# One written-out issue order for all engines over all eight batches, with loads held on named VectorE operations

## The chip, the cores and the metric

The kernel runs on one core of a Trainium2 chip. The metric is the device time of one execution in microseconds, the median of several. The profile shows one execution, with its own time.

## The reference

Attention without softmax, per batch (8) and head (8), with 576 positions and 64 features per head, and then a gated long convolution with a projection on either side. What is computed, in short:

```python
def phi(x, c, s):
    r = np.maximum(x, 0.0)
    return np.concatenate([r * c, r * s], axis=-1)
q_p, k_p = phi(q, cos_w, sin_w), phi(k, cos_w, sin_w)
kv = np.einsum('bhsf,bhsd->bhfd', k_p, v)
num = np.einsum('bhsf,bhfd->bhsd', q_p, kv)
den = np.einsum('bhsf,bhf->bhs', q_p, k_p.sum(2))[..., None] + 1e-06
x = (num / den).transpose(0, 2, 1, 3).reshape(B, S, H * D)
...
x1, x2, x3 = split(x @ w_proj)
x2_conv = irfft(rfft(x2, axis=1) * rfft(filter_fft, axis=0))
out = (x1 * x2_conv * x3) @ w_out
```

Inputs and output are fp32. All matmuls run in fp16 with fp32 sums.

## The kernel before

Every batch goes through the same steps. In the order of its data: loads of q, k and v (512 KB and 64 KB of each, cast to fp16 by transfers that POOL issues, into six buffers `raw`); phi, the features qp and kp (VectorE, DVE: one instruction of 2560 columns and five of 512 for q, ten of 512 for k); va, v beside ones (ScalarE, ACT, or DVE); kv (TensorE, PE); qt, the transpose of qp into the one buffer qpt (for batches 0 and 1 on PE, from batch 2 on by DMA transposes that SyncE, SP, issues); num (PE) with the division to att (DVE), in four parts of two heads; xt, the transpose of att (for batch 0 on PE, then by one DMA transpose on SP); fx (PE, evicted by ACT), which folds att for the projection to x2; x2 (PE, evicted to x2f by ACT) in three parts; dft, the transform of x2 by a table, in three parts of 32-column matmuls (PE), evicted to xf (ACT) and multiplied by the filter's spectrum (DVE: m, m, yf); the gate, in four parts, for each x0 and x2s (two groups of eight matmuls of 288 columns, each pair evicted by ACT) and their product g (DVE); inv, the inverse transform (PE, evicted to eq by ACT); y (six DVE operations for each of four parts: eo twice, y twice, times g, ye); out (PE, evicted to os by ACT) and its transfer on SP.

PE's results stand in PSUM tiles of one tag, "u", with four buffers, so a group of matmuls starts when the eviction of the fourth group before it has read its tile.

What sets the order is the code in two parts. The setup (tables by sines, the filter's spectrum h) and batches 0 to 2 are written out call by call in a manual schedule, where instructions stand as they are written. Then a loop from batch 2 on emits the steps of batch b, with num, xt and fx of b+1 and loads, phi, qt, va and kv of b+2 between them (the names `n` and `n + 1` in the code); `behind` puts phi and va of the next batch behind a marked instruction of this one in the issue order. A whole step is emitted at a time: `emit_qt(n + 1, x)` for four x puts four transposes side by side on SP, and `emit_input_dma` three loads side by side on POOL. Each part of x2 is followed by its eviction at once, and in the loop the matmuls of dft stand behind it.

Names in the rows: L574 is x2's matmul, L592 its eviction, L613 dft, L645 the gate, L505 num, L477 the transpose of qp, L553 that of att, L110 a feature of 512 columns, L142 the load of 512 KB, L683 to L693 y, L404 and L417 the filter's matmuls, L712 out.

Of the kernel before, what the change touches and what calls it, by code (L numbers as in the profile page):

```python
# [17 lines left out]
def kernel(  # L18
# [30 lines left out]

    A1 = 2048.0  # L50
# [47 lines left out]
    v32 = work.tile([128, NH, NJ * D], FP32, tag="qp", bufs=2, name="v32")  # L98
    qpt_buf = const("qpt", [128, NH, SP_], FP16)
    va_buf = [const(f"va{i}", [128, NH, NJ, 66], FP16) for i in range(2)]  # L100
    raw_buf = [const(f"raw{i}", [128, NH, NJ * D], FP16) for i in range(6)]

# [3 lines left out]
    def tsc(out, in0, s1, op0, s2=None, op1=None):  # L106
        if op1 is None:
            return nc.vector.tensor_scalar(out=out, in0=in0, scalar1=s1, scalar2=None, op0=op0)
        else:
            return nc.vector.tensor_scalar(out=out, in0=in0, scalar1=s1, scalar2=s2, op0=op0, op1=op1)  # L110
# [12 lines left out]
    def behind(*key):  # L123

        return tc.issue_after(mark[key].ins) if key in mark else nullcontext()


    raw_t = {}
    raw_n = [0]
    XT_DMA = (1, 2, 3, 4, 5, 6, 7)  # L130
    DMA_QT = 2

    def load_qk(b, nm, hs=slice(0, NH), after=None):
        src = {"q": q, "k": k, "v": v}[nm]
        if hs.start == 0:
            raw_t[(b, nm)] = raw_buf[raw_n[0] % len(raw_buf)]
            raw_n[0] += 1
        rw = raw_t[(b, nm)]
        load_rows(nc.gpsimd, rw, src, b, hs, after)

    def load_rows(queue, rw, src, b, hs, after=None):
        first = queue.dma_start(  # L142
            out=rw[:, hs, 0 : 4 * D],
            in_=src[b, hs, 0:NM].rearrange("h (p j) d -> p h (j d)", j=4),
        )
        mark["load", b] = queue.dma_start(
            out=rw[0:64, hs, 4 * D : 5 * D], in_=src[b, hs, NM:S].rearrange("h p d -> p h d")
        )

        if after:  # L150
            hold(first, after)

    def hold(ins, key):

        tc.add_manual_dep(
            ins.ins, mark[key].ins.name,
            mybir.DependencyInfo(mybir.DependencyClass.Sync, mybir.DependencyReason.DATA),
            reason="hold",
        )

    def emit_va(b, xs=range(4), copy=nc.scalar.copy):
        for x in xs:
            hs = slice(2 * x, 2 * x + 2)
            copy(
                out=va_buf[b % 2][:, hs, :, 0:D],
                in_=(raw_t[(b, "v")] if b else v32)[:, hs].rearrange("p h (j d) -> p h j d", j=NJ),
            )

    def emit_input_dma(b, after=None):
        load_qk(b, "q", after=after)  # L170
        load_qk(b, "k")
        load_qk(b, "v")

    def load_wp(w):
# [5 lines left out]
    def load_filter():  # L180
# [6 lines left out]
    def load_wo():  # L187
        nc.gpsimd.dma_start(out=wo16, in_=moe_w_out.rearrange("(i p) n -> p i n", p=128))

# [6 lines left out]
    def emit_iotas(part):  # L196
        if part < 0:
# [3 lines left out]
            ])  # L201
            return
        if part == 0:
# [3 lines left out]
            iota("er_i", [128, 4, 16], lambda t: [(t, [[1, 4], [4, 16]], 0, 0)])  # L207
            return
# [9 lines left out]
        iota("sr_i", [128, QS], lambda t: [(t, [[2, 2], [8, QS // 2]], 1, 0)])  # L218

    def emit_cols():  # L220
        nc.vector.memset(half_pi, PI / 2.0)
        nc.scalar.activation(
# [3 lines left out]
        p = cc["p"] = small("p")  # L226
        nc.vector.tensor_copy(out=p, in_=cc["p_i"])
        nc.vector.memset(v32[64:128, :, 4 * D : 5 * D], 0.0)
        for r in raw_buf[0:2]:
            nc.vector.memset(r[64:128, :, 4 * D : 5 * D], 0.0)  # L230
        for va in va_buf:
            nc.vector.memset(va[:, :, :, D : D + 2], 1.0 / A1)
        nc.vector.memset(warm, 0.0)
        m = cc["m"] = small("m")
        rnd(m, p, 1.0 / 16.0, -15.0 / 32.0)
        lo = small("lo")
        stt(lo, m, -16.0, p)
        m8 = small("m8")
        tsc(m8, m, 1.0 / 9.0, AL.mult, -8.0 / 9.0, AL.add)
        ph = small("ph", 8).rearrange("p (k c) -> p k c", c=2)  # L240
        tsc(ph, cc["kr_i"], m8, AL.mult)
        tsc(ph[:, :, 0], ph[:, :, 0], 0.25, AL.add)
        rr = small("ph_r", 8).rearrange("p (k c) -> p k c", c=2)
        tsc(rr, ph, RC, AL.add, -RC, AL.add)
        nc.vector.tensor_tensor(out=ph, in0=ph, in1=rr, op=AL.subtract)
        coef = small("coef", 9)
        nc.vector.memset(coef[:, 8:9], 1.0)
        nc.scalar.activation(
            out=coef[:, 0:8], in_=ph.rearrange("p k c -> p (k c)"), func=AF.Sin, scale=TWO_PI
        )  # L250
# [30 lines left out]
    def cos_of(dst, m):  # L281
# [3 lines left out]
        nc.scalar.activation(out=a, in_=m, func=AF.Abs, bias=m_half[0:nr])  # L285
        nc.scalar.activation(
# [3 lines left out]
    def emit_rows():  # L290
# [27 lines left out]
        mk = cc["mk"] = small("mk", 8)
# [445 lines left out]
    for w in (0, 2, 1):  # L764
        load_wp(w)
# [205 lines left out]
```

## Time and profile before

| | us |
|---|---|
| median of 3 timed runs | 273.61 (272.73 to 273.91) |
| the profiled execution | 275.25 |
| its span in the trace | 273.4 |
| its mean granted clock of PE | 0.926 |
| PE busy | 222.1 (81%) |
| DVE busy | 198.4 (73%) |
| ACT busy | 165.7 (61%) |
| POOL busy | 48.0 (18%) |

The span is the time from the first instruction to the last in the trace; the execution's own time has 1.85 us more around it. Busy times are sums over all stages. The share of an engine that bounds one stage is read from the windows, since the setup, the first batches, the steady batches and the end have different limits. The granted clock is given as a share of the full 2.4 GHz.

### The profile page before, as it was taken

The page shows a single profiled execution, that of the slowest core. Times are in us where ns is not written, and L with a number is a line of the kernel's source. Part 1 is how long each engine was busy: PE and PEld are TensorE (multiplying, and loading weights), DVE is VectorE, ACT ScalarE, POOL GpSimd, SP SyncE. Part 2 cuts the span into 40 slices and gives each one's busy share as a digit, 9 for nine tenths or more (in the row PEclk, how much of TensorE's full clock was granted, in tenths as well). Part 3 has the DMA queues.
Part 4 walks back from the last instruction along what each step waited for, and adds up shares of the span by engine and source line. Part 5 has one row for each costly group of instructions (what it writes and reads, how often), then busy time and mean ns, then how long its engine had stood idle before and what let it go on. Part 6 is the DMA issues. An engine that isn't in the chain of part 4 may idle for free.

```text
span 273.4 us, 5930 instructions
## 1 busy us (share of the span) xinstructions
PE 222.1 (81%) x2282; PEld 145.6 (53%) x2282; DVE 198.4 (73%) x665; ACT 165.7 (61%) x256; POOL 48.0 (18%) x75
## 2 busy tenths in 40 slices
PE   2755987869995840446999999999999999999990
PEld 0344865644684520213776686577658657745840
DVE  4988567997399990515788979897897868456661
ACT  2255599484963540022695778588677948857731
POOL 8933500201810281100024022000000000000000
PEclk9989799997998995575999999999999999999997
DMA  7999998099998499999587999996596134042204
GB/s 142 212 206 193 199 192 118 7 181 193 144 191 103 111 212 164 147 156 196 114 86 122 235 147 162 272 191 152 174 198 95 56 119 98 0 173 80 78 19 173
DMA packets 95612, 39.70 MB, mean 145 GB/s; under 512 B 63648, under 2 KB 91296, under 8 KB 95584
## 3 DMA queue, kind: packets, MB, share of 16 engines
q0 software_dynamic: 38464, 16.26, 49.1%
q1 hardware_dynamic: 56752, 22.49, 39.9%
q10 hardware_dynamic: 368, 0.59, 0.6%
q8 instruction: 17, 0.28, 0.4%
q14 instruction: 11, 0.09, 0.1%
HBM read 33.69 MB, written 9.44 MB: 158 GB/s over the span
## 4 chain that ended last, share of the span: by engine, by line
PE 57%; DMA 15%; DVE 13%; ACT 11%; issue 2%; SPq 1%; POOL 0%; DVEq 0%; ACTq 0%; POOLq 0%
PE x L645 20%; PE x L574 10%; PE out L712 9%; DMA qpt<-qp 9%; PE dft L613 3%; DMA v<-in_v_dram 3%; PE kv L465 3%; DVE att L515 3%; PE fx L532 3%; ACT x2f L592 2%; PE inv L662 2%; PE inv L666 2%; DMA raw<-in_k_dram 2%; PE num L505 2%; PE out L718 1%
## 5 line engine op out<-in xcount | busy, mean ns | idle before, releaser
L645 PE MATMUL x<-xt,wp 128*128 128x288 f16 x512 | 69.5, 292 | 0.7 <-ACT x0s L650 0.4
L645 PEld LDWEIGHTS <-wp 128*128 128x128 f16 x512 | 50.4, 100 | 16.4 <-issue 3.4
L592 ACT ACTIVATE x2f<-x 128x1024 f16<-128x1024 f32 (+1 forms) x24 | 21.1, 885 | 36.4 <-PE x L574 36.4
L574 PE MATMUL x<-wp,fx 128*128 128x512 f16 (+1 forms) x160 | 39.0, 410 | 2.2 <-ACT fx L543 1.7
L505 PE MATMUL num<-kvs,qpt 128*128 128x65 f16 x320 | 15.7, 203 | 23.7 <-DMA qpt<-qp 19.1
L712 PE MATMUL out<-wo,y 128*128 128x512 f16 x128 | 30.6, 387 | 2.6 <-ACT os L740 2.3
L652 DVE TENSOR_TENSOR g<-x0s,x2s 128x576 f16<-128x576 f16 x32 | 14.6, 455 | 22.0 <-ACT x2s L650 22.0
L505 PEld LDWEIGHTS <-qpt 128*128 128x128 f16 x320 | 13.4, 103 | 29.9 <-DMA qpt<-qp 21.2
L515 DVE TENSOR_TENSOR att<-num,rcp 128x640 f16<-128x640 f32 x32 | 26.4, 824 | 0.8
L650 ACT CAST x2s<-x 128x576 f16<-128x576 f32 x32 | 20.6, 643 | 10.5 <-PE x L645 10.5
L650 ACT CAST x0s<-x 128x576 f16<-128x576 f32 x32 | 20.6, 644 | 7.4 <-PE x L645 6.0
L511 DVE TENSOR_TENSOR rcp<-num,epsc 128x10 f32<-128x10 f32 x32 | 5.1, 161 | 25.9 <-PE num L505 25.6
L574 PEld LDWEIGHTS <-fx 128*128 128x128 f16 (+1 forms) x160 | 13.5, 105 | 19.5 <-issue 6.8
L615 ACT CAST xf<-dft 128x1024 f16<-128x1024 f32 (+1 forms) x24 | 18.9, 812 | 7.3 <-PE dft L613 7.3
L672 ACT CAST eq<-inv 128x576 f16<-128x576 f32 x32 | 18.5, 672 | 4.6 <-PE inv L666 4.6
L712 PEld LDWEIGHTS <-y 128*128 128x128 f16 x128 | 12.4, 99 | 15.1 <-issue 2.1
L142 POOL DMA_DIRECT2D raw<-in_q_dram x9 | 10.5, 1163 | 54.5 <-DVE qp L110 39.0
L662 PE MATMUL inv<-itab,yf 128*128 128x144 f16 x128 | 16.9, 232 | 2.8 <-DVE att L515 2.8
L543 ACT CAST fx<-fx 128x576 f16<-128x576 f32 x30 | 18.7, 647 | 0.0
L683 DVE TENSOR_TENSOR eo<-eq 128x288 f16<-128x288 f16 x64 | 17.6, 303 | 1.3 <-ACT eq L672 1.3
L743 ACT ACTIVATE os<-out 128x1024 f32<-128x1024 f32 x14 | 14.5, 1039 | 6.3 <-PE out L712 5.5
L465 PE MATMUL kv<-va,kp 128*128 128x65 f16 x320 | 13.2, 197 | 5.1 <-DVE kp L110 1.9
(156 smaller groups left out, 406.3 us busy)
## 6 DMA issues: line engine op xcount, KB each, us to landing
out_dram<-os SPq DMA_DIRECT2D x30, 256.0 KB, 2.8
raw<-in_q_dram POOLq DMA_DIRECT2D x7, 512.0 KB, 11.8
raw<-in_k_dram POOLq DMA_DIRECT2D x7, 512.0 KB, 11.6
raw<-in_v_dram POOLq DMA_DIRECT2D x7, 512.0 KB, 11.5
wp<-in_moe_w_proj_dram POOLq DMA_DIRECT2D x3, 512.0 KB, 10.1
v<-in_v_dram SPq DMA_DIRECT2D x2, 512.0 KB, 5.5
out_dram<-os SPq DMA_DIRECT2D x15, 64.0 KB, 4.1
filt<-in_moe_filter_fft_dram POOLq DMA_DIRECT2D x2, 288.0 KB, 12.6
```

Source lines behind the costliest of these rows:

```text
L465: nc.tensor.matmul(u[:, h // 4, ds((h % 4) * 65, 65)], kp[:, j, h].rearrange("p a b -> p (a b)"), va[:, h, j, 0:65], start=(j == 0), stop= ...
L505: nc.tensor.matmul(u[:, hh, ds(t * 65, 65)], qpt_buf[:, h, ds(t * 128, 128)], kvs[:, h // 4, ds((h % 4) * 65, 65)], start=True, stop=True,)
L515: mark["att", b, hp] = nc.vector.tensor_tensor(out=att[:, hp].rearrange("p t (h d) -> p h t d", h=2), in0=nv[:, :, :, 0:D], in1=rcp.unsque ...
L543: mark["fx", b] = copy(out=fx[:, c].rearrange("p (v t a) -> p t v a", t=4, a=16), in_=uf.rearrange("p (t v a) -> p t v a", t=4, a=16)[:, : ...
L574: nc.tensor.matmul(dst, fx[:, c, ds(128 * ch, n)], wp16[:, c, ds(DM, DM)], start=(c == cs[0]), stop=(c == cs[-1]),)
L592: mark["x2f", b, bl] = nc.scalar.mul(out=x2f[:, 2 * bl : 2 * bl + n], in_=u[:, 0:n], mul=X2SC)
L615: mark["xf", b, bl] = nc.scalar.copy(out=xf, in_=u[:, :, 0:n])
L645: nc.tensor.matmul(u[:, hf, 0:HS], wp16[:, i, ds(w * DM + c * 128, 128)], xt[:, i, ds(HS * hf, HS)], start=(i == 0), stop=(i == NC - 1),)
L650: mark[f"x{w}s", b, c] = nc.scalar.copy(out=x, in_=u[:, :, 0:HS])
L662: nc.tensor.matmul(u[:, comp, ds(par * QS, QS)], yf[par][:, comp, ds(c * 128, 128)], itab[:, par + 4 * comp], start=(par == 0), stop=False,)
L672: mark["eo", b, c] = nc.scalar.copy(out=eq.rearrange("p a b c -> p a (b c)"), in_=u[:, :, 0:HS])
L712: nc.tensor.matmul(u[:, x], y[:, c, ds(QS * t, 128)], wo16[:, c], start=(c == 0), stop=(c == NC - 1),)
```

## The change

The loop, the marks and `behind` go. Each step becomes a generator that yields after each instruction or small group (a group of matmuls, an eviction, one DVE operation), and one text of words says which generator goes on next, over all eight batches and the setup:

```diff
+    def run(plan, **batch):
+        for word in plan.format(**batch).split():
+            word, _, n = word.partition("*")
+            word, _, which[0] = word.partition("'")
+            key = word.lstrip("~")
+            name = key.rstrip("0123456789.")
+            if key not in open_steps:
+                open_steps[key] = step[name](*(int(x) for x in key[len(name) :].split(".") if x))
+            held[0] = last_dve[0] if word[0] == "~" else None
+            for _ in range(int(n or 1)):
+                next(open_steps[key])
```

`dft1.0` is one step of dft of batch 1, part 0; `*3` three steps; `'v` and `'a` put an eviction or a feature on DVE or ACT. A load with `~` waits for the DVE operation that was emitted last:

```diff
+    def load_rows(queue, rw, src, b, hs):
+        to = slice(0, rw.shape[1]) if rw.shape[1] < NH else hs
+        first = queue.dma_start(
+            out=rw[:, to, 0 : 4 * D],
+            in_=src[b, hs, 0:NM].rearrange("h (p j) d -> p h (j d)", j=4),
+        )
+        if held[0] is not None:
+            tc.add_manual_dep(
+                first.ins, held[0].ins.name,
+                mybir.DependencyInfo(mybir.DependencyClass.Sync, mybir.DependencyReason.DATA),
+                reason="hold",
+            )
...
-    for b in range(2, B + 1):
...
-        if n + 1 < B:
-            emit_input_dma(n + 1)
-            with behind("g", b - 1, NC - 1):
-                emit_phi(n + 1, "q")
-            for x in range(4):
-                emit_qt(n + 1, x)
...
+    run("""
+        Sk0.0 io1 io0 io2 pad0 pad3 pad2 cols ones0 th cols pk0.0 pk0.0'a pk0.0 th'v Lq0.0
...
+        pr1.1 dft1.2 dft1.0 kv2.2 dft1.2 ~Lq4.2 y0.2*3 pq3.2 dft1.2 y0.2 dft1.0 dft1.2 ga1.1
...
+        out7.2.1 out7.1.1*2 out7.0.1 y7.3 out7.0.1 out7.1.1 out7.2.1*3 out7.1.1*3
+    """)
```

(`pr` is x2, `ga` and `gb` are the two groups of the gate, `xp` is the PE transpose of att of batch 0, `S` a load on SP, `L` one on POOL.) Fifteen loads are held: v, q and k of batch 3, v, q, k of 4, v, k, q of 5, q, v, k of 6 and q, v, k of 7. The first halves of k and v of batch 0 come as fp32 by SP, into k32 and v32, and some of batch 0's features go to ACT. The narrow matmuls (the 64-column part of x2, the 32-column ones of dft, the 64-column part of out) are placed next to each other. The last batch's out is cut in two, so that both last groups of a part are issued before its eviction. Instructions: PE 4566 to 4554, DVE 612 to 602, ACT 250 to 261, POOL 75 to 76, SP 43 to 52.

What the change does to SP's queue, around the transposes of batches 3 and 4 (qp_1521 and qp_1933 before). Before:

```order
L745 DMA out_dram<-os_3_1482 128x512 x2
L733 DMA out_dram<-os_4_1511 64x256 x2
L477 DMA_TRANSPOSE qpt<-qp_1521 128x10x128 x4
L477 DMA_TRANSPOSE qpt<-qp_1933 128x10x128 x4
L553 DMA_TRANSPOSE xt_1721<-att_1630 128x20x128
L745 DMA out_dram<-os_1_1968 128x512 x2
L745 DMA out_dram<-os_3_1981 128x512 x2
L733 DMA out_dram<-os_4_1994 64x256 x2
L477 DMA_TRANSPOSE qpt<-qp_2383 128x10x128 x4
```

After, where qp_1238 is batch 3's and qp_1490 batch 4's:

```order
L570 DMA_TRANSPOSE qpt<-qp_1238 128x10x128 x4
L847 DMA out_dram<-os_0_1355 128x512 x2
L847 DMA out_dram<-os_0_1782 128x512 x2
L653 DMA_TRANSPOSE xt_1921<-att_1833 128x20x128
L570 DMA_TRANSPOSE qpt<-qp_1490 128x10x128
L837 DMA out_dram<-os_4_1641 64x256 x2
L570 DMA_TRANSPOSE qpt<-qp_1490 128x10x128
L847 DMA out_dram<-os_1_1377 128x512 x2
L570 DMA_TRANSPOSE qpt<-qp_1490 128x10x128 x2
L847 DMA out_dram<-os_1_1812 128x512 x2
```

Four transposes of a batch stand by themselves now with an out or two between them; before, those of batches 3 and 4 were eight in a row.

POOL's queue, from the load of w_out on (raw_ is one of the six buffers). Before:

```order
L188 DMA wo_87<-in_moe_w_out_dram 128x4x512
L142 DMA raw_100<-in_q_dram 128x8x256
L146 DMA raw_100<-in_q_dram 64x8x64
L142 DMA raw_97<-in_q_dram 128x8x256
L146 DMA raw_97<-in_q_dram 64x8x64
L142 DMA raw_98<-in_k_dram 128x8x256
L146 DMA raw_98<-in_k_dram 64x8x64
L142 DMA raw_99<-in_v_dram 128x8x256
L146 DMA raw_99<-in_v_dram 64x8x64
```

After:

```order
L193 DMA wo_87<-in_moe_w_out_dram 128x4x512
L149 DMA raw_98<-in_v_dram 128x8x256
L159 DMA raw_98<-in_v_dram 64x8x64
L149 DMA raw_96<-in_q_dram 128x8x256
L159 DMA raw_96<-in_q_dram 64x8x64
L149 DMA raw_100<-in_k_dram 128x8x256
L159 DMA raw_100<-in_k_dram 64x8x64
L149 DMA raw_101<-in_v_dram 128x8x256
L159 DMA raw_101<-in_v_dram 64x8x64
L149 DMA raw_97<-in_k_dram 128x8x256
```

The loads have the same sizes; each 128x8x256 one behind w_out in the second list is held on a DVE operation (v4, q4, k3, v5, k4), where the ones of before wait only for their buffer and for the queue.

DVE, where batch 3's k features begin. Before (kp_1532 is batch 3's, from buffer raw_98):

```order
L511 TENSOR_TENSOR rcp_3_1399<-num_3_1388,epsc 128x10
L514 RECIPROCAL rcp_3_1399<-rcp_3_1399 128x10
L515 TENSOR_TENSOR att_1305<-num_3_1388,rcp_3_1399 128x2x5x64
L108 TENSOR_SCALAR qp_1521<-raw_97 128x40x64
L110 TENSOR_SCALAR qp_1521<-raw_97,tcol 128x8x64 x5
L110 TENSOR_SCALAR kp_1532<-raw_98,ccol 128x8x64
L110 TENSOR_SCALAR kp_1532<-raw_98,scol 128x8x64
L110 TENSOR_SCALAR kp_1532<-raw_98,ccol 128x8x64
L110 TENSOR_SCALAR kp_1532<-raw_98,scol 128x8x64
```

After (kp_1451 is batch 3's, from raw_100). The load into raw_100 is held on the second m of xf_1_1313; behind it stand a reciprocal, an att and then these:

```order
L117 TENSOR_TENSOR yf_1_1360<-m_1_1_1337,m_1_1_1339 128x512 x2
L117 TENSOR_TENSOR rcp_2_1372<-num_2_1344,epsc 128x10
L610 RECIPROCAL rcp_2_1372<-rcp_2_1372 128x10
L117 TENSOR_TENSOR att_1309<-num_2_1344,rcp_2_1372 128x2x5x64
L117 TENSOR_TENSOR yf_2_1293<-m_1_2_1240,m_1_2_1245 128x128
L117 TENSOR_TENSOR rcp_3_1400<-num_3_1380,epsc 128x10
L610 RECIPROCAL rcp_3_1400<-rcp_3_1400 128x10
L117 TENSOR_TENSOR att_1309<-num_3_1380,rcp_3_1400 128x2x5x64
L117 TENSOR_TENSOR g_1205<-x0s_1_1291,x2s_1_1316 128x576
L117 TENSOR_TENSOR eo_0_1443<-eq_0_1413 128x4x72
L112 TENSOR_SCALAR qp_1238<-raw_99,tcol 128x8x64 x5
L112 TENSOR_SCALAR kp_1451<-raw_100,ccol 128x8x64
```

Before, phi of a batch follows in one piece behind the att of the batch before it; now its operations stand between yf, att, g and eo of three batches, and the first k feature comes 18 instructions behind the one that frees its load.

## Rows read from the trace of the kernel before

**Rows 1.** The page: busy time by engine; one DMA issue (KB each, us to landing)

```profile
PE 222.1 (81%) x2282; PEld 145.6 (53%) x2282; DVE 198.4 (73%) x665; ACT 165.7 (61%) x256; POOL 48.0 (18%) x75
...
v<-in_v_dram SPq DMA_DIRECT2D x2, 512.0 KB, 5.5
```

**Rows 2.** Windows: from:to, length, busy us of each engine, PEclk, DMA share, GB/s

```profile
0.00:16.60 16.60, 8.24 (x58) 4.05 (x58) 12.62 (x58) 3.66 (x8) 14.17 (x35) 1.00 1.09 182
...
97.00:129.40 32.40, 13.27 (x122) 6.50 (x121) 13.23 (x46) 5.73 (x7) 6.03 (x8) 0.65 1.37 166
...
146.58:170.72 24.14, 24.07 (x261) 16.24 (x260) 21.28 (x72) 18.14 (x28) 4.75 (x6) 1.00 1.31 183
170.72:194.87 24.15, 24.08 (x262) 16.27 (x260) 21.28 (x72) 18.14 (x28) 0.00 (x0) 1.00 0.99 196
...
241.77:273.40 31.63, 24.65 (x181) 13.78 (x180) 15.66 (x51) 16.56 (x27) 0.00 (x0) 0.96 0.31 109
```

**Rows 3.** Chain of waits in a steady batch: start us, us, what

```profile
174.83 1.03 ACT x2f L592
...
175.90 0.61 PE dft L613 x6
...
177.61 0.00 issue
...
180.45 1.96 PE x L645 x16
```

**Rows 4.** Timeline, 97 to 130 us: start, us, what, [idle before <-releaser]

```profile
97.78 31.18 SPq L477 DMA_TRANSPOSE qpt<-qp  x8
...
109.60 0.73 PE L505 MATMUL num<-kvs,qpt 128*128 128x65 f16 x10 [9.54 <-DMA qpt<-qp]
```

**Rows 5.** DMA issues from 97 to 127 us: KB each, median us to landing

```profile
raw<-in_q_dram POOLq DMA_DIRECT2D x2, 512.0 KB, 17.2
raw<-in_k_dram POOLq DMA_DIRECT2D x1, 512.0 KB, 13.3
raw<-in_v_dram POOLq DMA_DIRECT2D x1, 512.0 KB, 19.3
```

**Rows 6.** DMA issues from 52 to 60.4 us

```profile
raw<-in_q_dram POOLq DMA_DIRECT2D x1, 512.0 KB, 6.1
```

**Rows 7.** DMA issues from 137 to 170 us

```profile
raw<-in_k_dram POOLq DMA_DIRECT2D x2, 512.0 KB, 6.5
raw<-in_v_dram POOLq DMA_DIRECT2D x2, 512.0 KB, 9.3
...
raw<-in_q_dram POOLq DMA_DIRECT2D x1, 512.0 KB, 11.8
```

**Rows 8.** Timeline, 16 to 17 us, VectorE

```profile
16.37 0.27 DVE L110 TENSOR_SCALAR kp<-raw,scol 128x256 f16<-128x256 f16 x1
```

**Rows 9.** Timeline, PE: transposes of qp, filter's matmuls

```profile
41.47 1.28 PE L485 MATMUL qt<-ident,qp 128*128 128x128 f16 x20
...
50.33 0.81 PE L404 MATMUL h_ps<-feo,hc 96*128 96x512 f16 x3
...
54.19 0.35 PE L417 MATMUL h_ps<-filt,hs__501 96*32 96x128 f16 x12
```

**Rows 10.** Timeline, DVE: spacing of features and of y operations

```profile
94.20 0.34 DVE L110 TENSOR_SCALAR kp<-raw,ccol 128x512 f16<-128x512 f16 x1
...
94.47 0.34 DVE L110 TENSOR_SCALAR kp<-raw,scol 128x512 f16<-128x512 f16 x1
...
141.40 0.30 DVE L686 TENSOR_TENSOR y<-eo 128x288 f16<-128x288 f16 x1
141.62 0.30 DVE L687 TENSOR_TENSOR y<-eo 128x288 f16<-128x288 f16 x1
```

**Rows 11.** Timeline, the last 5 us: PE's last matmul and the last issue

```profile
268.35 0.38 PE L712 MATMUL out<-wo,y 128*128 128x512 f16 x1 [1.82 <-ACT os L740]
...
269.69 0.34 ACTq L741 DMA_DIRECT2D out_dram<-os  x1
```

More of the change, by code (lines that the diff above doesn't have):

```diff
@@ L97 @@
     feo = setupp.tile([NP, 2, 3, DM], FP16, tag="feo", name="feo")
-    v32 = work.tile([128, NH, NJ * D], FP32, tag="qp", bufs=2, name="v32")
+    k32, v32 = (
+        work.tile([128, 4, NJ * D], FP32, tag="att", bufs=2, name=f"{x}32") for x in "kv"
+    )
     qpt_buf = const("qpt", [128, NH, SP_], FP16)
@@ L131, with at @@
     DMA_QT = 2
[L133 to L141, printed above, removed]
+    HALF = (slice(0, 4), slice(4, 8), slice(0, 8))
+    held = [None]
+    def at(half):
+        return HALF[half]
+    def load_rows(queue, rw, src, b, hs):
+        to = slice(0, rw.shape[1]) if rw.shape[1] < NH else hs
@@ L161, in emit_va @@
[L161 to L174, printed above, removed]
+        if held[0] is not None:
[3 more added lines that the diff above has]
+                reason="hold",
+            )
@@ new lines, with step_pk @@
+    kp_t, qp_t, kvs_t, att_t, fx_t, xt_t, moe = {}, {}, {}, {}, {}, {}, {}
+    def step_pk(b, half):
+        hs = at(half)
+        rw = k32 if b == 0 and half == 0 else raw_t[(b, "k")]
+        if b not in kp_t:
+            kp_t[b] = work.tile([128, NJ, NH, 2, D], FP16, tag="kp", bufs=1, name=f"kp{b}")
+        for j in range(NJ):
+            for x, col in enumerate((ccol, scol)):
+                dst, src, c = kp_t[b][:, j, hs, x], rw[:, hs, ds(j * D, D)], col[:, j : j + 1]
+                if which[0] == "a":
+                    nc.scalar.activation(out=dst, in_=src, func=AF.Relu, scale=c)
+                else:
+                    tsc(dst, src, c, AL.mult, 0.0, AL.max)
+                yield
@@ L565 @@
-    moe = {}
-    def emit_x2(b, bls=range(3)):
-        fx = fx_t[b]
-        if 0 in bls:
-            moe.setdefault(b, {})["x2f"] = work.tile([128, 5, DM], FP16, tag="x2f", name=f"x2f{b}")
-        x2f = moe[b]["x2f"]
+        u = unit(f"fx{b}_{c}")
+        uf = u.rearrange("p a b -> p (a b)")
+        for t in range(4):
+            nc.tensor.matmul(
+                uf[:, ds(256 * t, 144)], att[:, c, t], fm.rearrange("p v a -> p (v a)"),
+                start=(t % 2 == 0), stop=False,
+            )
@@ L642, in emit_gate, with step_gate, gate @@
+    def step_gate(w):
+        def gate(b, c):
+            xt = xt_t[b]
             u = unit(f"x{w}_{b}_{c}")
@@ L747, in emit_warm @@
-    def emit_warm(n):
-        warm_up(unit("warm"), n)
-    HA, HB = slice(0, 4), slice(4, 8)
+                if cut and t < 4 and cs[0] > 0:
+                    yield
+            if not (cut and tiles[0] < 4 and cs[0] > 0):
+                yield
+        if grp == 2:
+            os_ = late["p"].tile([128, DM // 2], FP32, tag="os4", bufs=1, name=f"os{b}_4")
+            ev(os_, u[:, 0, 0 : DM // 2], OUTSC)
+            yield
+            for hf in range(2):
+                (nc.scalar if last and hf else nc.sync).dma_start(
+                    out=out[b, NM:S, ds(hf * (DM // 2), DM // 2)], in_=os_[ds(64 * hf, 64)],
+                )
+            yield
+            return
```

945 lines of the change are left out of this document (477 added, 468 removed).

## The prediction

> **What bounds the kernel now.** I read the page first: PE is busy for 222.1 of the 273.4 us and DVE for 198.4 [rows 1]. These are averages, so the second view was the windows, cut at the first matmul of each batch's x2. In a steady batch, 170.72 to 194.87, PE is busy for 24.08 of 24.15 us at full clock, and DVE for 21.28 [rows 2]: PE bounds it, with DVE close behind. Elsewhere PE waits: it is busy for 8.24 us of the first 16.6 and for 13.27 us of the 32.4 from 97 to 129.4, at a granted clock of 0.65 [rows 2].
>
> The third view was the chain of waits in the steady batch. What counts as busy hides one wait: an x2 matmul ends, ACT's eviction to x2f takes 1.03 us, and only then do the first dft matmuls start, 1.07 us after the eviction began [rows 3]. So PE works for 24.15 − 1.07 = 23.1 us a batch.
>
> The fourth view was the timeline of 97 to 130, to see what is late there. The transposes of qp (batches 3 and 4) stand behind each other on SP, which is busy issuing eight for 31.18 us, and each num waits for one: the first num waits 9.54 us [rows 4]. Of DMA issues in that stretch the 512 KB loads take 17.2, 13.3 and 19.3 us to land [rows 5]; one alone takes 6.1 [rows 6]. Four loads and eight transposes had been issued together.
>
> **PE's work, the base of the sum.** The change leaves the arithmetic of the eight batches alone, so I add it at the steady price: 8 × 23.1 = 184.8. Outside the steady batch come the PE transposes: 80 of qp (batches 0 and 1) and 20 of att (batch 0) at 1.28 / 20 = 0.064 us [rows 9]: 6.4. The filter's 12 wide matmuls at 0.81 / 3 = 0.27 and 72 narrow ones at 0.35 / 12 = 0.029 [rows 9]: 5.3. Sum 196.5. About 4 of it can be done before the start set below (half of kv, all of qt and half of num of batch 0): 192.
>
> **Start.** PE can't run on before the features of batch 0 exist. Before, the last k feature starts at 16.37 [rows 8], with 12.62 us of DVE work in that time [rows 2]. After, half of k comes by SP as fp32, as the first v did, which took 5.5 us [rows 1], so it is there at about 6. Of the 13.2 us of DVE work that the new list puts up to the last k feature, about 1.7 stands ahead of the first; ACT takes over some features. 6 + 11.5 gives 17.5; some of it overlaps, and I take 17 (15 to 18.5).
>
> **Tail.** Before, the last matmul starts at 268.35, after a wait of 1.82, and the span ends 5.05 later, with an eviction and a transfer [rows 11, 2]. In the new list both last groups of out7 stand ahead of their evictions, so that wait goes. Last PE work to end: 6.
>
> Base: 17 + 192 + 6 = 215.
>
> **The wait for x2f.** The new list puts other matmuls (gb, num, ga of another batch) between x2 and dft, where before only the wait stood. It costs 0 if they always cover the 1.03 us, 8 × 1.07 = 8.6 if never. In some places four narrow words do stand side by side: I take half, 4.
>
> **DVE's lead at the start.** From the last k feature to the last g of batch 0 the list holds 30.7 us of DVE work against 27.5 of PE work, by spacings such as 0.27 between two kp features and 0.22 between two y operations [rows 10]. PE must wait there for about the difference: 4 (0 to 6). Later DVE has about 141 us (152 by busy means) against PE's 148 up to the end of batch 7's features: it is hidden, but with little to spare.
>
> **The held loads.** These are the added wait. Fifteen loads wait for a named DVE operation; on their queue, POOL's, the next loads are behind, in the same order, so each is late by itself. What waits for one is DVE (phi, va), and behind DVE num's division and then PE. The DVE work between hold and first use, in us, by the list: v3 18, q3 5, v4 13, q4 13, k3 5, v5 16, k4 9, q6 21, q5 6.5, k5 12, v6 12, k6 8, q7 9, v7 33, k7 12. k3 shows it: 18 instructions between, three att and five qp features among them. Landing takes 6.5, 9.3 and 11.8 where loads are spread [rows 7], 13.3 to 19.3 in the crowd [rows 5], 6.1 alone [rows 6]. What exceeds the work between is waited for. At 6.5 that is 1.5 for q3 and for k3, 3 in all. At the mean of rows 7, (2×6.5 + 2×9.3 + 11.8) / 5 = 8.7, it is 3.7 + 3.7 + 2.2 (q5) + 0.7 (k6) = 10. At 11.8 it is 28, at 14.3 it is 53, at 16 it is 71. I take 10 (3 to 28), since spread loads are what the list makes.
>
> The transposes of qp are now single words between the outs, 6 to 22 us of DVE work ahead of their num where the old ones had none to spare; xt has 4 to 9. Alone or between outs they fit; I add 1 (0 to 6). The narrow matmuls, made adjacent: the first gate group behind dft takes 2.12 against 1.96 for the next [rows 3], so a change of shape costs at most 0.16, some 1.3 in all; I take 0 as the gate's row may have another reason. The k32 and v32 loads move from POOL to SP in a stretch where SP has nothing else. The 12 matmuls and 10 DVE rows fewer are below 1 us.
>
> **The sum.** 215 + 4 + 4 + 10 + 1 = 234 us. It is made on the span of one execution, 273.4, which took 275.25 with what lies around it; the timed median is 273.61. So the span stands for the median here. Against 273.4 the 39 us come from the 19 idle us in the window of 97 to 129.4, from the 8.4 that PE idles in the first 16.6, from the waits for x2f (4), the tail (2) and the lower granted clock around the stalls, less the new waits.
>
> **Rivals.**
> - *All in time.* If loads land as alone, DVE doesn't lead and the x2f waits are covered, it is 215 to 222. For it: the batch at 146 to 171 runs at 24.07 of 24.14 busy although loads and transposes fly [rows 2]. Against: three independent things must go well.
> - *Crowding stays.* DMA engines are shared: in 97 to 129.4 their share is 1.37 [rows 2] and everything lands late together. If held loads meet transposes in the same way once, num waits for qpt as before: 32.4 − 13.27 = 19 us of PE's time come back, giving 253 (250 to 272). The window at 146 to 171 with share 1.31 and no loss speaks against [rows 2]. The Trainium skill, "DMA: Bandwidth & Descriptors", section "Queues, rings and completion order", says that each DMA engine takes packets in turn from the queue rows that have work; by that, a hold moves a load but gives a transpose no priority over one in flight. By that rule the time is the one just given, 253; the rows of landing times (6.1 alone, 17.2 in company) agree that transfers share.
> - *Holds too late, slower than before.* If held loads land as in 97 to 127, 16 us on average, their waits are 71: 215 + 4 + 4 + 71 + 1 = 295. It decides from a mean landing of about 14 us on (53 us of waits, 277). Against: there, four loads had been issued within 9 us beside eight transposes; here a hold separates nearly each one.
> - *The change doesn't do what it says, or gains and losses cancel* (a fixed order that no engine can reorder, with DVE as the bound): about 273.
>
> **Chances.** Forecast (222 to 250) 0.68; all in time (213 to 222) 0.08; crowding 0.14; no change 0.03; holds too late 0.07. The range 216 to 260 leaves out the fastest part of the second (0.04), the slowest part of the third (0.04), and the last two: 0.18. The likeliest one's own range is 222 to 250. A difference under 0.5% this measurement can't tell from none; faster by more than that: 0.68 + 0.08 + 0.14 = 0.90, same 0.03, slower 0.07.
>
> **What would show it.** In the profile after: first gate matmul at about 26 to 29; PE's busy sum about 200 to 210 instead of 222.1, with a granted clock near 1.00 after 30 us; no num that waits several us for qpt; steady batches at 23 to 25 us each; DVE waiting for raw at q3, k3, q5 and k6, together about 10 us and none above 5; x2f waits in front of dft in about half of the batches. The forecast is wrong if loads take over 12 us to land, if SP's queue holds a transpose back behind an out whose eviction is late, or if PE's idle time names DVE in the steady batches, which would make DVE the bound.

## The result

The changed kernel takes 244.26 us (median of 4 runs, 243.49 to 248.27) against 273.17 for the kernel before in the same call: a ratio of 0.893, interval 0.889 to 0.897. The forecast was 234 with a range of 216 to 260. The profiled execution has a span of 242.5 (before 273.4). Some executions of a kernel are over 1.5% longer than its fastest: ratios and intervals leave those out, medians and ranges do not.

The page of the changed kernel, busy time by engine (answers to [rows 1]):

```profile
PE 210.4 (87%) x2276; PEld 142.2 (59%) x2276; DVE 193.1 (80%) x657; ACT 168.6 (70%) x268; POOL 46.4 (19%) x75
```

PE is busy 12 us less, at a mean granted clock of 0.961 instead of 0.926, and idles 32 us where it idled 51.

The waits that end idle time in the changed kernel, first PE's and then DVE's (who waits, for whom, us in total, times, longest):

```profile
PE qt L579 <- DVE qp L112: 7.1, 3, 5.5
PE num L599 <- DMA qpt<-qp: 6.7, 2, 3.7
PE x L731 <- DMA xt<-att: 4.3, 3, 1.8
...
PE dft L704 <- ACT x2f L137: 0.2, 1, 0.2
...
DVE qp L112 <- DMA raw<-in_q_dram: 3.5, 1, 3.5
DVE qp L112 <- DMA qpt<-qp: 3.1, 1, 3.1
...
DVE kp L112 <- DMA raw<-in_k_dram: 1.5, 2, 1.3
```

The first line falls before the last k feature of batch 0. The wait for x2f, which the chain of the kernel before has once a batch [rows 3], is gone. The waits for transposes are not.

Start and tail, from the timeline: the last k feature of batch 0 and PE's last matmul (answer to [rows 8, 11]).

```profile
18.95 0.27 DVE L112 TENSOR_SCALAR kp<-raw,scol 128x256 f16<-128x256 f16 x1
...
236.23 0.30 PE L822 MATMUL out<-wo,ye 128*64 128x256 f16 x2 [0.23 <-DVE ye L117]
```

**Where the time went, by stages.** I cut each run at the first x2 matmul of batches 1, 3 and 7. The last two columns are experiments (below) in which batches 3 to 7 are not loaded. The orders differ, so the work done by a cut differs by a few us too: the second stage has 585 matmuls of PE in the kernel before and 518 in the changed one, the third 1006 and 1050 (the two runs without loads).

| stage, us | before | changed | before, no loads | changed, no loads |
|---|---|---|---|---|
| to x2 of batch 1 | 60.8 | 56.9 | 59.9 | 56.3 |
| to x2 of batch 3 | 85.6 | 49.0 | 67.0 | 46.7 |
| to x2 of batch 7 | 95.3 | 106.1 | 95.3 | 93.5 |
| to the end | 31.7 | 30.5 | 31.8 | 30.4 |
| span | 273.4 | 242.5 | 254.0 | 226.9 |

The change gains 36.6 in the second stage and gives back 10.8 in the third. Windows of the changed kernel, one batch each from the first x2 matmul of batch 2 on, the last with two (columns as in [rows 2]):

```profile
83.30:105.90 22.60, 22.60 (x260) 15.89 (x259) 20.14 (x70) 16.95 (x27) 6.36 (x8) 1.00 1.32 194
105.90:136.50 30.60, 25.50 (x263) 16.68 (x261) 22.81 (x74) 17.99 (x28) 3.13 (x4) 0.94 1.17 184
136.50:165.10 28.60, 24.87 (x263) 16.93 (x261) 21.71 (x73) 17.93 (x28) 4.70 (x6) 0.94 1.11 174
165.10:212.00 46.90, 46.90 (x531) 32.85 (x529) 39.79 (x133) 36.40 (x58) 1.56 (x2) 1.00 0.78 147
```

PE never waits from 83 to 106 and from 165 to 212. In the 59 us between it idles 8.8, and the granted clock falls to 0.94: PE is busy for 50.4 us, where two batches without loads take 46.7 (below). The two together, 12.5, are what the third stage is longer by than without loads (106.1 against 93.5).

One of these waits in the timeline of the changed kernel:

```profile
113.91 4.23 SPq L570 DMA_TRANSPOSE qpt<-qp  x2
...
115.67 0.88 POOL L149 DMA_DIRECT2D raw<-in_k_dram  x1 [16.59 <-DVE y L117]
...
124.43 1.28 PE L599 MATMUL num<-kvs,qpt 128*128 128x65 f16 x20 [2.99 <-DMA qpt<-qp]
```

SP issues the last two transposes of a batch's qp at 113.9 and 115.4; POOL's load of k5 is released at 115.67, and num waits 2.99 us, to 124.43, for the second transpose, which took 9.0. The list leaves that transpose no slack: in the run without loads (below) it is issued at 110.96 and lands at 115.78, and num starts at 115.82. The other wait of num, 3.7, ends at 148.35 with a transpose issued at 140.46 that took 7.8. Both follow directly behind another transpose on SP, not behind an out with a late eviction.

### The profile page after: what moved, and what is told of

It reads as the page before. It is cut to its first block, busy times and chain, and to the rows that moved or that the text cites. A ratio compares the mean times of both kernels' runs of the same rounds, so it can differ in the third digit from the quotient of the medians.

```text
span 242.5 us, 5900 instructions
## 1 busy us (share of the span) xinstructions
PE 210.4 (87%) x2276; PEld 142.2 (59%) x2276; DVE 193.1 (80%) x657; ACT 168.6 (70%) x268; POOL 46.4 (19%) x75
## 3 DMA queue, kind: packets, MB, share of 16 engines
q1 hardware_dynamic: 56752, 22.49, 46.7%
## 4 chain that ended last, share of the span: by engine, by line
PE 57%; DVE 16%; DMA 14%; ACT 6%; SPq 3%; issue 2%; ACTq 0%; DVEq 0%
PE x L731 21%; PE out L816 10%; PE x L673 9%; DMA qpt<-qp 7%; DMA xt<-att 5%; PE num L599 3%; PE inv L760 3%; PE inv L764 3%; DVE qp L112 3%; DVE att L117 3%; PE kv L556 2%; DVE kp L112 2%; PE fx L627 2%; SPq L570 2%; PE dft L704 2%
## 5 line engine op out<-in xcount | busy, mean ns | idle before, releaser
L731 PE MATMUL x<-xt,wp 128*128 128x288 f16 x512 | 72.3, 289 | 5.0 <-DMA xt<-att 4.3
L731 PEld LDWEIGHTS <-wp 128*128 128x128 f16 x512 | 48.9, 99 | 21.4 <-DMA xt<-att 5.4
L673 PE MATMUL x<-wp,fx 128*128 128x512 f16 (+1 forms) x160 | 34.5, 387 | 0.0
L137 ACT ACTIVATE os<-out 128x1024 f32<-128x1024 f32 (+1 forms) x22 | 17.5, 795 | 17.6 <-PE out L816 15.7
L673 PEld LDWEIGHTS <-fx 128*128 128x128 f16 (+1 forms) x160 | 13.5, 101 | 15.6 <-issue 2.4
L137 ACT CAST eq<-inv 128x576 f16<-128x576 f32 x32 | 20.1, 649 | 2.0 <-PE inv L764 1.8
L599 PEld LDWEIGHTS <-qpt 128*128 128x128 f16 x320 | 13.5, 101 | 10.6 <-DMA qpt<-qp 7.3
L149 POOL DMA_DIRECT2D raw<-in_k_dram x8 | 7.0, 878 | 62.7 <-DVE y L117 55.0
L760 PE MATMUL inv<-itab,yf 128*128 128x144 f16 x128 | 18.0, 232 | 0.6 <-DVE yf L117 0.6
L117 DVE TENSOR_TENSOR y<-eo 128x288 f16<-128x288 f16 x64 | 17.6, 301 | 0.4
L764 PE MATMUL inv<-itl,yf 128*128 128x288 f16 x64 | 17.5, 294 | 0.0
L117 DVE TENSOR_TENSOR yf<-m,m 128x512 f16<-128x512 f16 (+1 forms) x48 | 15.5, 349 | 0.7
```

Source lines behind the costliest of these rows:

```text
L117: last_dve[0] = nc.vector.tensor_tensor(out=out, in0=in0, in1=in1, op=op)
L137: return nc.scalar.copy(out=out, in_=in_) if mul is None else nc.scalar.mul(out=out, in_=in_, mul=mul)
L149: first = queue.dma_start(out=rw[:, to, 0 : 4 * D], in_=src[b, hs, 0:NM].rearrange("h (p j) d -> p h (j d)", j=4),)
L599: nc.tensor.matmul(u[:, hh, ds(t * 65, 65)], qpt_buf[:, h, ds(t * 128, 128)], kvs[:, h // 4, ds((h % 4) * 65, 65)], start=True, stop=True,)
L673: nc.tensor.matmul(dst, fx[:, c, ds(128 * ch, n)], wp16[:, c, ds(DM, DM)], start=(c == cs[0]), stop=(c == cs[-1]),)
L731: nc.tensor.matmul(u[:, hf, 0:HS], wp16[:, i, ds(w * DM + c * 128, 128)], xt[:, i, ds(HS * hf, HS)], start=(i == 0), stop=(i == NC - 1),)
```

## The experiments

"Theory" in the expectations is the one named there. Ratios are against the kernel before in the same call; the changed kernel's own is 0.893 (0.889 to 0.897). Waits and spans are of one profiled execution each.

**1. No load held.** All fifteen `~` are taken off.

```diff
-        qt1.2 tf*4 ti pk1.2 qt1.2'a pk1.2*2 ~Lv3.2 pk1.2*3 fx0.2'v pk1.2*2 qt1.0'a rows
+        qt1.2 tf*4 ti pk1.2 qt1.2'a pk1.2*2 Lv3.2 pk1.2*3 fx0.2'v pk1.2*2 qt1.0'a rows
```

> The changed kernel with none of its fifteen loads held: each goes as soon as its buffer is free and its turn comes on POOL's queue. Theory (the holds keep loads away from the DMA transposes, and cost 5 us of DVE's waits for raw in the changed kernel): loads bunch, the transposes of qp and att beside them take 8 to 15 us to land instead of 3.5, num and the gate wait for them, 248 to 258 us. Rival (the holds are only a wait that was added): the waits of 5 us for raw go and nothing comes in their place, 238 to 241 us. Second rival (the buffers' own waits already set the times, a hold changes little): 243 to 246 us.

Measured: 253.46 us, ratio 0.922 (0.911 to 0.933). The waits, PE's and DVE's:

```profile
PE num L599 <- DMA qpt<-qp: 6.6, 1, 6.6
PE x L731 <- DMA xt<-att: 6.1, 2, 4.3
PE x L731 <- ACT os L137: 2.6, 1, 2.6
...
DVE qp L112 <- DMA qpt<-qp: 7.0, 1, 7.0
```

By the ratios the holds bring 8 us (0.922 against 0.893 of 273), so they are not only an added wait. The time lies in the theory's range, but its mechanism is shown in part only. Six transposes of qp run beside loads for at least nine tenths of their time, with holds as without; 9 are clear of loads with holds and 15 without, as the loads then come in bunches. What is worse without holds is the longest: 14.0 us instead of 10.1. PE's waits for transposes are 12.7 us instead of 11.0, and a wait of 2.6 for an eviction of out is new.

**2. Every hold 4 us later.** Each `~L` word is put behind 4 us more of DVE work.

```diff
-        ga4.0 y3.2 dft4.2 y3.1 ~Lv7.2 dft4.2 y3.0 dft4.0 dft4.2 pq6.2 dft4.2 dft4.0*2 qt5.0
+        dft4.0 num5.0 pq6.2 ~Lq7.2 y3.3 dft4.1 gb4.0 va6.2'v num5.0 ~Lv7.2 gb4.0 ga4.0
```

> The changed kernel with every held load put 4 us of DVE work later in the list, so that its hold ends 4 us later; nothing else moves. Theory of the forecast (what a landing exceeds the DVE work between hold and first use is waited for): at the landing of about 8.5 us seen in the changed kernel, with 4 us less between, q3, k3, q5, k4, k6 and q7 are late by 7 + 7 + 6 + 3 + 4 + 3 = 30 us in all instead of some 6, so 24 more: 262 to 272 us. Rival (PE has other work in its queue behind the late features, so most of the lateness is hidden): 245 to 252 us.

Measured: 274.82 us, ratio 1.006 (1.001 to 1.011): 30.6 more than the changed kernel, all of the gain, and more than either range of the expectation. PE's wait for transposes of att, and DVE's waits for raw:

```profile
PE x L731 <- DMA xt<-att: 23.5, 3, 13.6
...
DVE kp L112 <- DMA raw<-in_k_dram: 17.7, 4, 8.1
DVE qp L112 <- DMA raw<-in_q_dram: 12.1, 2, 6.4
...
DVE qp L112 <- issue: 7.9, 1, 7.9
```

The table of DVE work is borne out in sum: held loads are waited for 29.6 us, where landing minus the work between gave 30. By load it is q3 5.7 (forecast 7), k3 7.6 (7), q5 7.9 (6), k4 1.6 (3), k6 0.4 (4) and q7 6.4 (3). q5's wait is the line with "issue": its 64 KB piece lands at 138.29, and the feature starts at 138.37. The longest wait, 8.1, is for a load that isn't held, k of batch 2: it stands on POOL's queue behind v3, whose hold ends at 45.45 instead of 33.19, and lands at 62.83 instead of 46.88. PE doesn't hide this lateness, but its longest wait, 13.6, has another cause: the transpose of batch 1's att, issued at 50.05 as soon as att is there, takes 18.5 us beside the loads of v3, v2, k2 and w_out.

**3. Narrow matmuls apart.** 25 narrow groups are moved behind the next wide one; PE changes its shape 61 times instead of 41 (runs of one shape 62 against 42).

```diff
-        va6.0 pr4.2 pr4.1 dft4.2 dft4.0 out2.2 kv5.2 y3.2 dft4.1 y3.1 g3.2 dft4.2 ~Lq7.2
+        pr4.2 pr4.1 out2.2 kv5.2 y3.2 y3.1 g3.2 dft4.2 ~Lq7.2 ga4.0 dft4.2 y3.2 dft4.2 y3.1
```

> The changed kernel with the narrow matmuls moved apart: 25 groups (32-column dft, 64-column x2 and out) are moved behind the next group of wide ones, so that PE goes 62 times from one shape to another instead of 42. Theory (a switch costs at most 0.16 us, 20 more cost up to 3): 244 to 247 us. Rival (adjacency is a large part of the gain): 250 us or more. If it is the same within 0.5%, adjacency is worth nothing that can be measured.

Measured: 242.18 us, ratio 0.888 (0.880 to 0.897). No loss shows, nor the 1 to 3 us of the theory: adjacency is worth nothing that these runs can measure.

**4 and 5. The kernel before with loads held.** First batch 4's (in effect only the 512 KB load of its q):

```diff
-            emit_input_dma(n + 1)
+            emit_input_dma(n + 1, ("att", n, 3) if b == 2 else None)
```

> The kernel before with one change: the loads of batch 4 wait for the last att of batch 3, so that the transposes of batch 3's qp no longer run beside four loads. Theory (the 19 idle us of PE between 97 and 129 come from transposes that share the DMA engines with loads): most of the stall goes, 258 to 264 us, and the transposes of batch 3 land in 3.5 to 5 us. Rival (the stall moves: batch 4's features are late by as much, and its transposes with them): 270 to 276 us.

Measured: 282.00 us, ratio 1.034 (1.027 to 1.041). That is above both ranges. The loads of the crowd were not batch 4's; this one only made batch 4 late:

```profile
PE num L505 <- DMA qpt<-qp: 24.9, 6, 9.6
```

One load of the kernel before was held already: q of batch 3 waits for a transpose of batch 2's qp, and not only for its buffer and the queue. In the kernel before:

```profile
POOL raw L142 <- DMA qpt<-qp: 13.0, 1, 13.0
```

Then the loads that were in flight, each of the three of batches 5 and 6 in both its pieces:

```diff
-            emit_input_dma(n + 1)
+            emit_input_dma(n + 1, ("att", 3, 3) if b in (3, 4) else None)
...
-        load_qk(b, "k")
-        load_qk(b, "v")
+        load_qk(b, "k", after=after if b > 3 else None)
+        load_qk(b, "v", after=after if b > 3 else None)
...
             hold(first, after)
+            if b > 3:
+                hold(mark["load", b], after)
```

> The kernel before with the loads that really were in flight in its stall held: those of batch 5 and 6 wait for the last att of batch 3; the order of every engine is as before. (In the run that held batch 4 it was the wrong loads: those landing beside the transposes were batch 5's three and batch 6's q.) Theory (the stall of 19 us comes from transposes of qp that share the DMA engines with four loads): the first four transposes land in 3.5 to 6 us, num of batch 3 waits 3 us or less in all, the loads land late by nothing that DVE waits for, 254 to 261 us. Rival (the stall has another cause, or the held loads make batch 5 late by as much): 268 to 276 us.

Measured: 266.65 us, ratio 0.968 (0.961 to 0.976), between the two ranges. All waits of num for qpt were 19.1 us in the kernel before. Most of that is gone, and part of it comes back at xt:

```profile
PE x L647 <- DMA xt<-att: 5.1, 1, 5.1
PE num L507 <- DMA qpt<-qp: 4.0, 3, 1.5
```

**6. dft right behind x2.** Each dft's matmuls and eviction follow the x2 eviction that they read.

```diff
-        va6.0 pr4.2 pr4.1 dft4.2 dft4.0 out2.2 kv5.2 y3.2 dft4.1 y3.1 g3.2 dft4.2 ~Lq7.2
+        pk5.2 y3.3 kv5.2*2 va6.0 pr4.2 dft4.2*2 pr4.1 dft4.1*2 dft4.0*2 out2.2 kv5.2 y3.2
```

> The changed kernel with each dft's matmuls and their eviction put right behind the eviction of the x2 parts that they read, as in the kernel before; nothing else moves. Theory (the new list's other work between x2 and dft hides the 1.07 us of the x2f eviction, 8 times): the wait comes back, PE waits 6 to 9 us for x2f, 248 to 253 us. Rival (PE's order is not what bounds the batches now, the DMA transposes do, so PE's waits elsewhere shrink by as much): 243 to 246 us.

Measured: 264.04 us, ratio 0.951 (0.940 to 0.962): 20 more than the changed kernel, above both ranges. Three of PE's waits:

```profile
PE dft L704 <- ACT x2f L137: 12.5, 10, 2.1
...
PE num L599 <- DMA qpt<-qp: 5.9, 2, 3.1
PE dft L704 <- ACT xf L137: 2.7, 3, 1.1
```

The profiled execution has a span of 258.2, 15.7 more. 12.3 of it are the wait for x2f, more than the 8.6 that I had as the worst case, and 2.7 a new wait of dft for the eviction of xf. The other changes (qpt and xt less, yf and kvs more) nearly cancel.

**7. Four holds tuned.** q5 ahead of q6 and earlier, q6, k5 and v7 later.

```diff
-        dft2.2 dft2.1 dft2.2 y1.3 dft2.0 qt3.2 y1.3 gb2.0 g2.0 dft2.2 ~Lq6.2 dft2.0 qt3.3
-        num3.1 out1.1 dft2.1 ~Lq5.2 out0.0 out1.1 num3.0 out1.0 num3.2 num3.1*2 num3.0*2
+        dft2.2 dft2.1 ~Lq5.2 dft2.2 y1.3 dft2.0 qt3.2 y1.3 gb2.0 g2.0 dft2.2 dft2.0 qt3.3
...
+        num3.3 y2.0*2 y2.1*2 inv2.2 inv2.3 y2.0 va5.2'v g2.1 num3.3*3 ~Lq6.2 xt3 y2.1 qt4.3
```

> The changed kernel with four of the fifteen holds moved, so that no load is released beside a transpose that num waits for, and none with less than 8 us of DVE work to its first use where its buffer allows: q5 4 us earlier and ahead of q6, q6 8 us later, k5 4 us later, v7 15 us later (in DVE work). Theory (landing in company costs PE its waits: 6.7 us for qpt and 3.5 us of DVE's for q5 in the changed kernel): 237 to 241 us. Rival (those waits are hidden, or come back at the next transpose): 243 to 246 us.

Measured: 259.41 us, ratio 0.945 (0.937 to 0.952): 15 more, above both ranges. I moved loads to where DVE had time for them, and so beside other transposes: ten of qp's now run beside loads for at least nine tenths of their time, where it was six. Its timeline:

```profile
105.20 3.07 SPq L653 DMA_TRANSPOSE xt<-att  x1
105.45 0.88 POOL L149 DMA_DIRECT2D raw<-in_q_dram  x1 [10.12 <-DVE att L117]
...
114.87 1.36 PE L731 MATMUL x<-xt,wp 128*128 128x288 f16 x8 [3.98 <-DMA xt<-att]
```

q6 now starts with the transpose of att, and the gate waits 3.98 for that one, which took 9.6.

**8. Outs issued by ACT.** `nc.sync` becomes `nc.scalar` for the transfers of out of batches 0 to 6.

```diff
-                nc.sync.dma_start(out=ov[tiles[i]], in_=os_[:, i])
+                nc.scalar.dma_start(out=ov[tiles[i]], in_=os_[:, i])
```

> The changed kernel with the transfers of out of batches 0 to 6 issued by ACT instead of SP, so that SP holds transposes alone. Theory of the queue (transposes of qp stand on SP behind outs that wait for their evictions, 36 us of such waits in the changed kernel): num's and the gate's waits for transposes, 11 us, shrink, 237 to 241 us. Rival (they are late because they share the DMA engines, not the queue, and ACT pays 0.4 us for each of 45 issues): 243 to 248 us.

Measured: 263.43 us (258.43 to 265.20), without a ratio; its lowest time is 14 above the changed kernel's median, above both ranges. The waits of the execution of 265.20, PE's and ACT's:

```profile
PE num L599 <- DMA qpt<-qp: 8.9, 2, 8.6
...
ACT os L137 <- DMA out_dram<-os: 10.2, 3, 6.6
```

With SP's queue free of outs, num's waits for transposes did not shrink. That speaks against the theory of the queue; the case is weak, as ACT got new waits.

**9 and 10. Both kernels without the loads of batches 3 to 7.** These batches work on data of batches 1 and 2; the order of all other engines is that of the kernel it comes from.

```diff
-            load_rows(nc.gpsimd, raw_t[(b, nm)], {"q": q, "k": k, "v": v}[nm], b, at(half))
+            if b < 3:
+                load_rows(nc.gpsimd, raw_t[(b, nm)], {"q": q, "k": k, "v": v}[nm], b, at(half))
```

> The changed kernel without the loads of q, k and v of batches 3 to 7 (these batches work on the data of batches 1 and 2; the order of every other engine is the same). So nothing is late for want of a load, and no transpose shares the DMA engines with one. Theory (what keeps the changed kernel above the sum of 215 are loads, late themselves or beside transposes): the waits for qpt (6.7), raw (5) and part of those for xt (4.3) go, and the slow clock behind them: 224 to 231 us. Rival (the order itself makes PE wait, for ACT, DVE and SP's queue): 236 to 243 us.

> The kernel before without the loads of q, k and v of batches 3 to 7 (these batches work on data of batches 1 and 2; the order of every other engine is the same). Theory (the stall of 97 to 129 is loads beside transposes): no num waits more than 3 us for qpt, the steady batches keep their 24.1 us, 248 to 257 us. Rival (eight transposes in a row on SP are the stall by themselves): 264 us or more.

Measured: the changed one 231.18 us (229.47 to 231.97, and one execution of 535.19), ratio 0.844 (0.837 to 0.850); the one before 256.15, ratio 0.936 (0.929 to 0.942). By span, loads cost the kernel before 273.4 − 254.0 = 19.4 and the changed one 242.5 − 226.9 = 15.6. With no loads the changed kernel is still 27.1 ahead. The ratios give about 17.5, 13.5 and 25, so each of these is good to some 2 us.

In the kernel before, without loads, the eight transposes that took SP 31.18 us to issue [rows 4] still stand in a row, and take 14.55:

```profile
95.34 14.55 SPq L478 DMA_TRANSPOSE qpt<-qp  x8
```

num's waits for qpt are 3.9 us in all (below) instead of 19.1. So the stall was the loads beside the transposes (the theory), and not the row of eight (the rival). Windows of the changed one without loads, from the first x2 of batch 3 to that of 4, and on to that of 7:

```profile
103.00:126.50 23.50, 23.39 (x262) 15.90 (x261) 21.00 (x70) 17.81 (x28) 0.00 (x0) 1.00 0.94 197
126.50:196.50 70.00, 70.00 (x791) 49.11 (x789) 61.33 (x205) 54.34 (x85) 0.00 (x0) 1.00 0.58 131
```

PE doesn't wait there at all: 70.0 / 3 = 23.3 us a batch, bounded by PE. Windows of the one before without loads, from the first x2 of batch 1 to that of 2, to that of 3, and one steady batch:

```profile
59.90:94.70 34.80, 28.71 (x293) 19.17 (x294) 29.17 (x100) 22.95 (x37) 0.00 (x0) 0.95 0.38 82
94.70:126.90 32.20, 28.16 (x298) 18.12 (x295) 26.73 (x95) 18.71 (x29) 0.00 (x0) 0.89 0.69 133
126.90:151.03 24.13, 24.05 (x266) 16.25 (x263) 21.26 (x71) 18.15 (x28) 0.00 (x0) 1.00 0.57 132
```

In the first two PE idles 10 us and runs at 0.95 and 0.89, with nothing loaded: this is the old order itself. PE's longest waits in these two:

```profile
PE num L506 <- DMA qpt<-qp: 3.9, 2, 2.6
PE inv L663 <- DVE att L516: 2.8, 2, 2.3
PE kv L466 <- ACT va L165: 1.7, 1, 1.7
PE x L575 <- ACT fx L544: 1.7, 3, 1.4
```

**11. q5 right ahead of q6.**

```diff
-        dft2.2 dft2.1 dft2.2 y1.3 dft2.0 qt3.2 y1.3 gb2.0 g2.0 dft2.2 ~Lq6.2 dft2.0 qt3.3
+        dft2.2 dft2.1 dft2.2 y1.3 dft2.0 qt3.2 y1.3 gb2.0 g2.0 dft2.2 ~Lq5.2 ~Lq6.2 dft2.0
```

> The changed kernel with one held load moved: q5 is put right ahead of q6 on POOL's queue and held on the same DVE operation as q6, some 2.5 us earlier than now. Theory (q5 lands late by 3.5 us, which DVE waits for, because q6, which is needed 20 us later, goes first): the 3.5 us go, 240 to 243 us. Rival (earlier by that much it lands beside other transposes, or what follows waits for the same transposes anyway): 244 to 250 us.

Measured: 244.62 us, ratio 0.887 (0.881 to 0.894). Not told apart from the changed kernel, so the 3.5 us did not come back as time. DVE's waits:

```profile
DVE qp L112 <- DMA qpt<-qp: 6.9, 1, 6.9
...
DVE qp L112 <- DMA raw<-in_q_dram: 3.8, 2, 2.0
```

The wait of 3.5 for q5 itself is gone (the two that are left are at other places, 1.8 and 2.0 us); DVE's wait for a transpose to have read qp grows from 3.1 to 6.9.

**12. Features of batch 0 on DVE.** `pk0.0'a` becomes `pk0.0`, five times (the expectation says four).

> The changed kernel with the four features of k of batch 0 that ACT computes given back to DVE; order as it is. Forecast's step on the start (PE's start is set by the last k feature of batch 0, by DVE's work up to it): four features of 0.27 to 0.58 us more on DVE, the end 1 to 2 us later, 245 to 247 us. Rival (the start is set by the chain behind it, num, att, xp, fx): no difference, 243.5 to 245 us.

Measured: 245.67 us, ratio 0.895 (0.887 to 0.904). The times don't tell it from the changed kernel. In its trace the last k feature is at 20.03 instead of 18.95, the first gate matmul at 25.4 instead of 23.8, and the span ends at 243.8 instead of 242.5. The later start is as the forecast's step has it; the 1.3 us at the end lie within what executions of one kernel differ by.

**Transposes beside loads, in all traces.** For each DMA transpose I took the time from its issue to its landing, and whether a load of q, k or v on POOL's queue was in flight in that time: "no load" is for at most 0.3 us of it, "the whole time" for at least nine tenths. Over the kernel before, the changed one and the twelve experiments:

```
transposes of qp       count  median us  longest
no load in flight        177       3.64      5.6
for part of the time      80       3.91     13.4
the whole time            79       9.83     15.6
transposes of att
no load in flight         60       4.99      7.4
for part of the time      29       6.17     18.5
the whole time             9      10.0      16.9
```

In the changed kernel 6 of 24 transposes of qp run wholly beside loads, 8.8 us in the median; in the kernel before 9, 11.8 us. With no loads of batches 3 to 7 the median is 3.6 in the changed order and 3.7 in the old one, 5.2 the longest, with all outs still under way: so it is the loads. The Trainium skill, "DMA: Bandwidth & Descriptors", section "Queues, rings and completion order", would have them share in turns; the rows agree that they share, and show the price.

## Why the prediction was right, and which of its steps were not

The direction and the range held; the kernel is 10 us slower than the forecast, and several steps stood for the wrong thing. That the total is no further off is in part luck: the wait for x2f came out 3.8 lower and the waits for raw 5 lower, and the transposes took more than both.

- **The base.** PE's 23.1 us a batch came out as 23.3 where nothing waits: 2 more in all. The tail of 6 is 242.5 − 236.2 = 6.3. The last k feature, put at 17, starts at 18.95. The 4 for DVE's lead is right in size: PE's waits from 19.2 to 56.9, those for the DMA of xt left out, sum to 4.0. But only 1.4 of them name DVE (att and yf); the others are ACT's evictions. The 1.07 that I took off for x2f was misread, though: PE does not stand still for it. In the kernel before, between the start of the eviction at 174.83 and dft at 175.90, thirteen matmuls of num (0.03 us each) and two of dft start, so about half of it (an estimate from these rows) is work:

```profile
174.63 0.47 PE L505 MATMUL num<-kvs,qpt 128*128 128x65 f16 x10
...
175.03 0.39 PE L613 MATMUL dft<-x2f,fcos 128*32 128x512 f16 x2
...
175.35 0.48 PE L505 MATMUL num<-kvs,qpt 128*128 128x65 f16 x10
```

- **The x2f wait** was 4 and is 0.2. That the new list covers it is shown: uncovered (experiment 6) it is 12.5, and the span 15.7 longer.
- **Without loads** my terms give 215 + 4 + 4 + 1 = 224; the span measured is 226.9; with the base and the x2f wait as measured they still give 224. So 2 to 3 us stand in no term; PE's waits for xt, of which 2.3 are left without loads, are part of that.
- **The held loads** were 10 and the transposes 1; loads cost 15.6. The lateness itself was overrated: DVE waits 5.0 for raw, not 10, with median landings of 8.4 to 10 us as forecast (one held load, v7, took 14.6, and nothing waited for it). The table of DVE work between hold and use stands in sum: 4 us less gave 29.6 us of waits for held loads where it says 30, single entries up to 4 off. "Each is late by itself" does not hold: there v3's hold made k2, which isn't held, land 16 us later. The step that failed is "Alone or between outs they fit; I add 1 (0 to 6)": the transposes are not alone. Loads run beside them, six of qp's 24 then take 8.8 us (median) instead of 3.6, and PE waits 6.7 for qpt and 4.3 for xt; without loads it is 0 and 2.3. Nor did the 6 to 22 us of DVE work ahead of num give slack everywhere: the transpose of 115.36 has none even without loads. This is the rival of crowding, in part: not once 19 us, but in several pieces.
- **Where the gain comes from** was put wrong. I ascribed the 39 us first of all to the 19 idle us of the stall. Loads cost 19.4 before and 15.6 now: the change gives back most of that stall further on, from 106 to 165 us. What it gains, 27.1 us with no load in either, is the order, together with the earlier k and the cut last out: 3.6 to x2 of batch 1, 20.3 from there to x2 of batch 3, 1.8 and 1.4 in the last two stages. In the 67.0 us that fall to 46.7 PE idled 10.1 and now 0.6, as the old code, written out call by call, left it waiting in turn for transposes, att, va and fx. The other 10.8 are busy time, in part work that the changed kernel has in other stages, in part a clock of 0.92 instead of 1.00; these two I can't separate. I had read most of that stretch (30 to 97 us) only as an average.
- **Narrow matmuls:** taken as 0, measured as 0.
- **The signs.** Right: PE's busy sum (200 to 210 named, 210.4), no wait for raw above 5, a tail without PE's wait of 1.82. Wrong: the first gate matmul at 23.8, not 26 to 29; num does wait for qpt, 3.0 and 3.7; two batches of 30.6 and 28.6, not 23 to 25, with a clock of 0.94 in them where it was to be near 1.00; no x2f waits rather than some; DVE waits for raw at q5 (3.5) and k3 (1.3), not at q3 and k6.
- **Slower than before if holds come too late:** not so here. Experiment 2 comes back to the time of the kernel before with holds 4 us later, by late loads and by a transpose beside bunched loads. The rival's mean landing of 16 us is 16.8 by its rows [rows 5], which makes its waits 81 and not 71.

What stays open: which words of the new order bring how much of the 27.1, by what way the holds bring their 8, and whether the time lost to loads (15.6) can be won without loss elsewhere; experiments 7 and 11 tried and didn't.

No version with all its loads was clearly faster than the changed kernel: the intervals of 3, 11 and 12 overlap its own.

## What to carry to other kernels

Before a stall is booked as gain, take its cause out of both kernels (here, the loads) and look at what the order is worth without it: most of the loads' cost stayed, and the order paid. A load has a time that is too late for its consumer and also places that are wrong for its neighbours; DVE slack alone doesn't choose well, as the run with four tuned holds shows. A held load also holds back what stands behind it on its queue. In a fixed order with its bounding engine busy for 87% of the span, fifteen holds that end 4 us of DVE work later cost 30 us, so change one word at a time and measure each.

## What the runs showed of the hardware that was not expected

- DMA transposes suffer much from company: 3.64 us in the median with no load in flight and 9.83 beside loads (qp). The 512 KB loads go from 6.1 alone [rows 6] to medians of 8.4 to 10 in the changed kernel, beside transposes or not.
- The granted clock falls where PE waits, but not in step with the idle time: 0.94 in the two batches with 5.1 and 3.7 us idle, 1.00 in those without, 0.89 in a stretch of 32.2 us with 4.0 idle (experiment 10) and 0.95 in one of 34.8 with 6.1.
- Giving SP's outs to ACT made ACT wait: 10.2 us, in the one execution traced, in which evictions stood until an out's transfer had freed its buffer.
